# RetNet attention and a maxout FFN in one kernel: another order of the operand sums, and fewer of them between two plain products

## The chip, the cores and the metric

The kernel runs on one core of a Trainium2 chip. The metric is the device time of one execution in microseconds (us); a kernel's time is the median of several runs. The core has a matrix engine (TensorE, PE in the profile; its weight loads are listed as PEld), a vector engine (VectorE, DVE), a scalar engine (ScalarE, ACT), a general engine (GpSimd, POOL) and a queue engine that starts most transfers (SyncE, SP). Each engine works through its own instructions in the order in which the program gives them; between engines, and within one where a value is passed on, they wait on semaphores.

## What is computed

Eight sequences of 576 positions with 8 heads of 64 go through a retention step (scores with a decay by distance, no softmax). Its result, 4608 rows of 512, goes through a feed-forward layer whose hidden value is the largest of three products.

```python
scores = scale * np.matmul(q, k.transpose(0, 1, 3, 2))
ret = scores * Dmat[None, :, :, :]             # Dmat = gamma ** (i - j) for j <= i, else 0
x = (ret @ v) as (B*S, H*D)                    # 4608 x 512
h = np.maximum(np.maximum(x @ w1, x @ w2), x @ w3)   # 4608 x 768
out = h @ w_out                                # 4608 x 512
```

The four weights come in as 64-bit floats and are turned into 32-bit ones on the chip.

## The kernel before

Rows are handled in 36 chunks of 128, and four chunks make a tile of 512 rows; there are nine tiles, t = 0 to 8. While the feed-forward layer of tile t is computed (`ffn(t)`, a generator), the attention of tile t + 1 is worked in between (`steps(t + 1)`, a list of twelve stations; after each the generator goes on to its next `yield`). The order of the instructions on each engine is thus written out by the program.

The hidden value has six blocks (`fb`, 128 columns each), in three pairs (`fp`).

- Tile 0 uses plain products: `up_plain` (L610) makes x times one weight for one block; the first of three is copied to h by ScalarE (L615), the others are joined by a maximum on VectorE (L614). The output is made by `downs_plain` (L597). The weights are converted along the way.
- Tiles 1 to 8 use a scheme with fewer products: for each block, the 24 products of half-size operands are replaced by 20 products of *sums* of operands (`PRODUCTS`, L65, matmuls at L587). They form five chains A to E that add up in five PSUM banks' tiles: A and B take turns in one pair of banks (`ps_x`), E, C and D in another pair (`ps_y`), so that C of a block takes the bank used two before it, and D the bank of E. ScalarE copies the running values out (L572), VectorE joins them (L567).
- In tile 1 the blocks run in the order 2, 3, 0, 1, 4, 5, and blocks 2 and 3 are still plain (`plain`): the sums of the weights aren't ready. Block 3's plain products use `ps_y`.

The sums of operands are written as lists. `X_SUMS` (13 sums of parts a11 to a24 of x, once for each tile from 1 on) and `W_SUMS` (19 sums of parts b11 to b43 of the weights, once for each pair fp, in place or into n1 to n8) are worked one by one by `combine` (L346), each one VectorE operation on 128x256 values. A third set, the sums of w_out (`sums_of_outs`, L378), has three times two VectorE operations (L386, L387) and two POOL operations (L390, L391).

Two queues hold work that is given out bit by bit: `chores` (the sums of weights and of w_out) and `urgent` (what `soon` puts there from tile 1 on: masks of scores, sums of x, transposes, loads; and the sums of hidden values). `chore(n)` takes the next n entries, urgent ones first. `weight_sums(fp)` puts the 19 sums of a pair and one marker into `chores`; tile 1 begins with pairs 0 and 2 there, and pair 1 follows when blocks 2 and 3 are made. In the plain blocks of tile 1, `ffn` gives out a fixed number of chores after each of the three plain products:

```python
for step, cost in enumerate(steps_of_one):
    if fb in plain:
        chore(8)
```

`up_plain_all` has the maximum of a product right behind the product and ahead of these chores. In tile 0, after the down products of blocks 3, 4 and 5, `chore(2)` gives out the sums of w_out; a `yield` after blocks 1 and 3 lets the attention's stations in. The last of these holds the step that makes x of tile 1 (`values`, xT, L184), followed by the 13 sums of x.

Of the kernel before, what the change touches and what calls it, by code (L numbers as in the profile page):

```python
# [53 lines left out]
FILL = 224  # L54
PARTS = 20

X_SUMS = """s19 = a12 + a14, s15 = s19 - a22, s3 = a22 - a12, s10 = s3 - a13, s13 = a12 + a13, s20 = s10 + a23,
            s14 = a24 - s15, s11 = s20 + a24, s11 = a21 - s11, s7 = s11 - s13, s6 = s19 + s7,
            s16 = a11 - s11, s16 = s16 - a14"""
W_SUMS = """b33 = b13 + b33, n1 = b13 + b43, n2 = n1 - b41, n3 = b11 - n2, n4 = b33 - b32, b43 = b43 + n4,  # L60
            b23 = b43 - b23, b43 = b41 - b43, n5 = b22 + b23, b41 = b41 - n5, b21 = b21 - b41,
            b23 = b32 + b23, b22 = b22 - b21, b32 = b22 - b32, n6 = b31 + n2, n7 = b42 + n4,
            b42 = b42 - n5, b31 = b31 + b32, n8 = b12 - n4"""

PRODUCTS = """E a11 b12, E a14 b42, B s15 n5, A a22 b21, C s3 b23, B s19 b41, A s10 b32, C a13 b31, B s6 n2, A s13 b22,  # L65
              C a11 b11, B s14 n1, A s11 n4, D s7 b43, B a23 n6, A s20 b33, D s16 b13, B a21 n3, A a21 n8, A a24 n7"""
# [6 lines left out]
         "A7": [("A1", ("A1", "B6"), ALU.add), ("A1", ("A1", "A5"), ALU.max), ("hi", ("A1", "A7"), ALU.max)]}  # L73
X_SUMS, W_SUMS = ([x.split() for x in text.split(",")] for text in (X_SUMS, W_SUMS))
PRODUCTS = [x.split() for x in PRODUCTS.split(",")]
# [4 lines left out]
def kernel(  # L80
# [93 lines left out]
    def chore(n=1):  # L174
        for _ in range(n):
            if urgent or chores:
                (urgent or chores).popleft()()  # L177

    def soon(step):

        if spread:
            urgent.append(step)
        else:
            step()  # L184
# [34 lines left out]
    def transposes(g):  # L219
        both = qks[g] = {}  # L220
        if g >= BY_PE:
            for n in ("k", "q"):
                t = both[n] = att.tile([P, NP, C], FP32, tag=n + "T", name=n + "T", bufs=2 if n == "k" else 3)
                soon(partial(nc.vector.transpose, t[:].rearrange("a p c -> a (p c)"),
                             raws.pop(("kx" if n == "k" else n, g))[:].rearrange("a p b i -> a (p b i)")))
            return
        for n, src in (("k", raws["k", g]), ("q", raws.pop(("q", g)))):
            pool, tag = (ps_r, "r") if g >= CPT else (ps_x, "x")
            pt = pool.tile([P, NP, C], FP32, tag=tag, name=n + "t")
            for p in range(NP):  # L230
                nc.tensor.transpose(pt[:, p, :], pair(src, p), ident[:C, :C])
            t = both[n] = att.tile([P, NP, C], FP32, tag=n + "T", name=n + "T", bufs=2 if n == "k" else 3)
            nc.scalar.copy(t[:], pt[:])
# [88 lines left out]
    def output(chunks, o, t, i):  # L322
# [9 lines left out]
        if i == CPT - 1 and t > 0:  # L332
# [4 lines left out]
            def step(n, dst, _, a, sign, b):  # L337
                combine(*(xS[t][x] for x in (dst, a, b)), sign)
                if dst not in (later[0] for later in X_SUMS[n + 1:]):
                    made[t].add(dst)  # L340

            for n, line in enumerate(X_SUMS):
                soon(partial(step, n, *line))

    def combine(dst, a, b, sign):
        nc.vector.tensor_tensor(dst, a, b, op=ALU.add if sign == "+" else ALU.subtract)  # L346
# [191 lines left out]
    def weight_sums(fp):  # L538

        def step(dst, a, sign, b):  # L540
            combine(*(factor(n, slice(2 * fp, 2 * fp + 2)) for n in (dst, a, b)), sign)

        for dst, _, a, sign, b in W_SUMS:
            chores.append(partial(step, dst, a, sign, b))
        chores.append(partial(summed_fp.add, fp))

    def late_room():
        pool = late["pool"]
        late["W"] = [pool.tile([P, NF, P], FP32, name=f"n{n}") for n in range(1, 9)]
        late["X"] = {n: pool.tile([P, NH], FP32, name=n)[:] for n in sorted({x[0] for x in X_SUMS})}  # L550

    converting = convert_all()

    def convert(n):
        for _ in range(n):
            next(converting, None)
# [35 lines left out]
    def downs_plain(t, h):  # L592

        ps = [(ps_x, ps_y)[m % 2].tile([P, DM], FP32, tag="xy"[m % 2], name="down") for m in range(NT // P)]
        for fb in range(NF):
            for m, b in enumerate(ps):
                nc.tensor.matmul(b[:], lhsT=h[:, fb, m * P:(m + 1) * P], rhs=w_sb["out", fb],  # L597
                                 start=(fb == 0), stop=(fb == NF - 1))
                if fb == NF - 1:
                    osb = opool.tile([P, DM], FP32, tag="osb", name="osb")  # L600
                    nc.scalar.copy(osb[:], b[:])
                    nc.sync.dma_start(out[t * NT + m * P:t * NT + (m + 1) * P, :], osb[:])
            yield

    def up_plain(t, h, fb, i):
        ps = (ps_x, ps_y)[fb % 2].tile([P, NT], FP32, tag="xy"[fb % 2], name="up")
        first_of_all = t == 0 and (fb, i) == (0, 0)
        for cols in (slice(0, NT - C), slice(NT - C, NT)) if first_of_all else (slice(0, NT),):
            for dc in range(NDC):
                nc.tensor.matmul(ps[:, cols], lhsT=w_sb[i, fb][:, dc * P:(dc + 1) * P], rhs=xT[t][:, dc, cols],  # L610
                                 start=dc == 0 and cols.start == 0, stop=dc == NDC - 1,
                                 skip_group_check=first_of_all)
        if i > 0:
            return lambda: nc.vector.tensor_tensor(h[:, fb, :], h[:, fb, :], ps[:], op=ALU.max)  # L614
        return lambda: nc.scalar.copy(h[:, fb, :], ps[:])  # L615

    def ffn(t):

        h = hpool.tile([P, NF, NT], FP32, tag="h", name="h")
        if t == 0:  # L620
            for fp, i in units:
                for fb in (2 * fp, 2 * fp + 1):
                    maximum = up_plain(t, h, fb, i)
                    if CPT not in qks:
                        maximum()
                        transposes(CPT)
                        convert(4)
                        continue
                    convert(4)
                    maximum()  # L630
                yield
            convert(6)
            for fb, _ in enumerate(downs_plain(t, h)):
                convert(4 if fb < 2 else 4 * len(pieces))
                if fb == 2:
                    while_converting.close()
                    late["pool"] = ctx.enter_context(tc.tile_pool(name="late", bufs=1))
                    late_room()
                    sums_of_outs()
                elif fb > 2:  # L640
                    chore(2)
                if fb in (1, 3):
                    yield
            yield
            return
        if t == 1:
            spread.append(True)
            weight_sums(0)
            weight_sums(2)
        plain = (2, 3) if t == 1 else ()  # L650
        order = (2, 3, 0, 1, 4, 5) if t == 1 else (0, 1, 4, 5, 2, 3)
        total = sum(24 if fb in plain else len(PRODUCTS) for fb in order)
        count = parts = 0
        for n, fb in enumerate(order):
            if fb not in plain:
                while fb // 2 not in summed_fp:
                    chore()
            steps_of_one = up_plain_all(t, h, fb) if fb in plain else up(t, h, fb)
            for step, cost in enumerate(steps_of_one):
                if fb in plain:  # L660
                    chore(8)
                elif step % 2 or step % 5 == 4:
                    chore(len(urgent) > 0)
                elif step % 4 == 2 and chores:
                    chores.popleft()()
                count += cost or 1
                if count * (NF // 2 * 3) >= (parts + 1) * total:
                    parts += 1
                    yield
            if n % 2:  # L670
                sums_of_hidden(h, fb // 2)
                if fb in plain:
                    weight_sums(fb // 2)
        chore(len(urgent))
        for n, _ in enumerate(downs(t, h)):
            chore(4)
            if n in (1, 3):
                yield
        yield

    def up_plain_all(t, h, fb):
        for i in range(3):
            up_plain(t, h, fb, i)()
            yield 8
# [85 lines left out]
    for t in range(N // NT):  # L770
        work = ffn(t)
        for todo in steps(t + 1):
            for step in todo:
                step()
            next(work, None)
# [51 lines left out]
```

## Time and profile before

| | |
|---|---|
| median of 7 runs | 777.7 us (777.42 to 778.01) |
| the profiled execution | 777.75 us, span 776.0 us |
| granted TensorE clock | 0.999 |
| TensorE matmuls | 767.3 us busy, 5032 instructions |
| VectorE | 568.2 us busy, 1249 instructions |
| ScalarE | 325.9 us busy, 811 instructions |
| GpSimd | 102.0 us busy, 124 instructions |
| tile 0 | to about 123.4 us of the span |
| plain blocks of tile 1 | 123.4 to 146.2 us |

The span runs from the first to the last instruction of the program. Lines of the profile name a kernel line (L346), an engine, an operation, and the tiles that are written and read. In a list by time the first number is the start in us, the second the length; "x2" joins instructions that follow each other, and brackets give the idle time just before and what ended it. In a list of waits the numbers are the total in us, the times and the longest. Lines on one source line list the count and the shortest, median and longest duration in ns. Starts on VectorE can overlap the end of the instruction before by some 0.08 us, so the distance from start to start is what an instruction costs there.

### The profile page before, as it was taken

To read this page: it belongs to the slowest core of one execution; us is meant where nothing else is said; L and a number is where in the kernel's file an instruction comes from. 1 tells how busy PE (TensorE), PEld (TensorE's weight loads), DVE (VectorE), ACT (ScalarE), POOL (GpSimd) and SP (SyncE) were. 2 spreads that over 40 slices of the span, in tenths; PEclk is the share of its full clock that TensorE was granted. 3 is DMA by queue.
4 is the path that set the end of the run, shared out by engine and by line. 5 is a ranking of instruction groups with operands and counts; after the bars stand their busy time and mean duration, and the time that the engine had idled before them with its cause. 6 is when DMAs were issued, how large, how long until landed. Compare 5 with 4: busy or idle time off the path is not lost.

```text
span 776.0 us, 14508 instructions
## 1 busy us (share of the span) xinstructions
PE 767.3 (99%) x5032; PEld 626.3 (81%) x5032; DVE 568.2 (73%) x1249; ACT 325.9 (42%) x811; POOL 102.0 (13%) x124
## 2 busy tenths in 40 slices
PE   8999999999999999999999999999999999999998
PEld 7545454688888888888888888888888888888887
DVE  3998979889677857785769657875778567855672
ACT  3665631154154514452345234532544054524651
POOL 2210112111102201111111111110111001200000
PEclk9999999999999999999999999999999999999999
DMA  9995543333233332343223333333333324001001
GB/s 221 238 233 129 158 112 102 58 58 59 85 57 58 58 75 54 60 82 65 61 54 59 58 96 59 56 60 95 58 56 58 77 50 77 6 15 41 2 1 54
DMA packets 237082, 59.33 MB, mean 76 GB/s; under 512 B 217936, under 2 KB 235728, under 8 KB 237008
## 3 DMA queue, kind: packets, MB, share of 16 engines
q1 hardware_dynamic: 236432, 58.07, 34.7%
q8 instruction: 39, 0.64, 0.4%
q10 hardware_dynamic: 576, 0.33, 0.1%
q14 instruction: 35, 0.29, 0.1%
HBM read 48.89 MB, written 9.44 MB: 75 GB/s over the span
## 4 chain that ended last, share of the span: by engine, by line
PE 93%; DVE 4%; DMA 2%; SPq 1%; issue 0%; ACT 0%; DVEq 0%; ACTq 0%
PE a L587 18%; PE b L587 15%; PE dx L427 11%; PE up L610 8%; PE c L587 8%; PE dz L427 5%; PE d L587 5%; PE e L587 5%; PE s L242 4%; PE o L298 4%; PE dy L427 3%; PE down L597 2%; PE o L311 2%; PE kv L262 2%; DVE w L346 1%; DMA qraw<-in_q_dram 1%
## 5 line engine op out<-in xcount | busy, mean ns | idle before, releaser
L567 DVE TENSOR_TENSOR part<-part 128x256 f32<-128x256 f32 x460 | 207.8, 460 | 80.2 <-ACT part L572 72.5
L572 ACT COPY part<-a 128x256 f32<-128x256 f32 x276 | 102.7, 372 | 85.0 <-PE a L587 73.1
L572 ACT COPY part<-b 128x256 f32<-128x256 f32 x230 | 85.6, 372 | 125.5 <-PE b L587 113.7
L610 PE MATMUL up<-xT,w 128*128 128x512 f32 (+2 forms) x200 | 84.7, 578 | 0.7 <-DVE w L516 0.7
L213 POOL TENSOR_TENSOR vd<-vraw,gk 128x512 f32<-128x512 f32 x36 | 40.8, 1132 | 325.6 <-DMA vraw<-in_v_dram 155.4
L587 PE MATMUL a<-s,w 128*128 128x256 f32 x276 | 82.3, 380 | 0.0
L587 PE MATMUL b<-s,n 128*128 128x256 f32 x276 | 82.1, 379 | 0.0
L610 PEld LDWEIGHTS up<-xT,w 128*128 128x128 f32 x200 | 36.8, 190 | 42.8 <-issue 38.7
L587 PEld LDWEIGHTS b<-s,n 128*128 128x128 f32 x276 | 52.4, 190 | 7.1
L587 PEld LDWEIGHTS a<-s,w 128*128 128x128 f32 x276 | 52.3, 190 | 7.3 <-issue 0.2
L587 PE MATMUL c<-xT,w 128*128 128x256 f32 x184 | 56.0, 386 | 0.0
L587 PE MATMUL b<-xT,n 128*128 128x256 f32 x184 | 55.4, 382 | 0.0
L587 PE MATMUL d<-s,w 128*128 128x256 f32 x184 | 55.2, 382 | 0.0
L587 PE MATMUL e<-xT,w 128*128 128x256 f32 x184 | 47.2, 379 | 0.0
L587 PE MATMUL a<-xT,n 128*128 128x256 f32 x184 | 47.2, 379 | 0.0
L567 DVE TENSOR_TENSOR h<-part 128x256 f32<-128x256 f32 x92 | 42.2, 458 | 6.6
L427 PE MATMUL dx<-To,H 128*128 128x256 f32 (+1 forms) x204 | 44.9, 370 | 0.0
L434 ACT COPY part<-dx 128x256 f32<-128x256 f32 (+1 forms) x34 | 10.5, 363 | 80.1 <-PE dx L427 77.9
L177 DVE TENSOR_TENSOR xT<-o,gq 128x512 f32<-128x512 f32 x28 | 18.1, 686 | 33.4 <-PE o L311 33.4
L427 PEld LDWEIGHTS dx<-To,H 128*128 128x128 f32 x204 | 36.6, 190 | 5.5 <-issue 1.0
L271 POOL TENSOR_TENSOR state<-state,gs 128x256 f32<-128x256 f32 x24 | 18.4, 765 | 170.3 <-DVE state L270 170.3
L242 PEld LDWEIGHTS s<-qT,kT 64*128 64x128 f32 x576 | 33.8, 188 | 7.9 <-PE b L587 4.0
(104 smaller groups left out, 1301.9 us busy)
## 6 DMA issues: line engine op xcount, KB each, us to landing
bits<-in_moe_w_dram SPq DMA_DIRECT2D x36, 256.0 KB, 5.1
out_dram<-osb SPq DMA_DIRECT2D x35, 256.0 KB, 2.1
kraw<-in_k_dram SPq DMA_DIRECT2D x32, 256.0 KB, 2.9
vraw<-in_v_dram SPq DMA_DIRECT2D x32, 256.0 KB, 3.4
qraw<-in_q_dram SPq DMA_DIRECT2D x464, 16.0 KB, 1.8
kxraw<-in_k_dram SPq DMA_DIRECT2D x464, 16.0 KB, 1.8
bits<-in_moe_w_out_dram SPq DMA_DIRECT2D x6, 512.0 KB, 4.2
qraw<-in_q_dram SPq DMA_DIRECT2D x6, 256.0 KB, 4.7
```

What stands on the lines that cost most here:

```text
L177: (urgent or chores).popleft()()
L213: nc.gpsimd.tensor_tensor(t[:], raws.pop(("v", g))[:], gk[:].unsqueeze(2).to_broadcast([C, H, D]), op=ALU.mult)
L242: nc.tensor.matmul(s[j][:, p, :], lhsT=kT[r, p, :], rhs=qT[r, p, :], start=True, stop=True)
L262: nc.tensor.matmul(kvs[g][half(h % 2), h // 2, :], lhsT=kr[r:, h, :], rhs=vds[g][r:, h, :], start=True, stop=True)
L271: nc.gpsimd.tensor_tensor(t[:], t[:], gs[:], op=ALU.mult)
L298: nc.tensor.matmul(o[n % 2][half(c), m, n // 2, :], lhsT=vds[g][:, h, :], rhs=sts[g][:, h % 2, h // 2, :], start=m == 0 and n < 2, stop=be ...
L311: nc.tensor.matmul(o[n % 2][half(c), m, n // 2, :old], lhsT=states[g][r, h // 2, :], rhs=qks[g]["q"][r, h // 2, :old], start=False, stop=True,
L427: nc.tensor.matmul(o, lhsT=hS[n](fp)[:, m * P:(m + 1) * P], rhs=late["T"][n][:, fp, cols], start=first and fp == 0 and (m == 0 or last and ...
L567: nc.vector.tensor_tensor(out, a, b, op=op)
L572: nc.scalar.copy(t[:], ps[step[0]][:])
L587: nc.tensor.matmul(ps[chain][:], lhsT=factor(w, fb), rhs=xS[t][x], start=n == 1, stop=ends, skip_group_check=True)
L610: nc.tensor.matmul(ps[:, cols], lhsT=w_sb[i, fb][:, dc * P:(dc + 1) * P], rhs=xT[t][:, dc, cols], start=dc == 0 and cols.start == 0, stop= ...
```

## The change

The entries of both lists are put in another order; the same 13 and 19 sums are made. In tile 0 the six entries of the sums of w_out are given out as 4, 0 and 2 after blocks 3, 4 and 5, where it was 2, 2 and 2. In tile 1, after the second plain product of block 3 (the last plain product but one), 4 chores are given out in place of 8.

```diff
-X_SUMS = """s19 = a12 + a14, s15 = s19 - a22, s3 = a22 - a12, s10 = s3 - a13, s13 = a12 + a13, s20 = s10 + a23,
-            s14 = a24 - s15, s11 = s20 + a24, s11 = a21 - s11, s7 = s11 - s13, s6 = s19 + s7,
-            s16 = a11 - s11, s16 = s16 - a14"""
-W_SUMS = """b33 = b13 + b33, n1 = b13 + b43, n2 = n1 - b41, n3 = b11 - n2, n4 = b33 - b32, b43 = b43 + n4,
-            b23 = b43 - b23, b43 = b41 - b43, n5 = b22 + b23, b41 = b41 - n5, b21 = b21 - b41,
-            b23 = b32 + b23, b22 = b22 - b21, b32 = b22 - b32, n6 = b31 + n2, n7 = b42 + n4,
-            b42 = b42 - n5, b31 = b31 + b32, n8 = b12 - n4"""
+
+X_SUMS = """s19 = a12 + a14, s3 = a22 - a12, s15 = s19 - a22, s10 = s3 - a13, s13 = a12 + a13, s20 = s10 + a23,
+            s14 = a24 - s15, s11 = s20 + a24, s11 = a21 - s11, s7 = s11 - s13, s16 = a11 - s11, s6 = s19 + s7,
+            s16 = s16 - a14"""
+W_SUMS = """b33 = b13 + b33, n1 = b13 + b43, n4 = b33 - b32, n2 = n1 - b41, b43 = b43 + n4, n3 = b11 - n2,
+            b23 = b43 - b23, n7 = b42 + n4, n5 = b22 + b23, b43 = b41 - b43, b41 = b41 - n5, b23 = b32 + b23,
+            b21 = b21 - b41, b42 = b42 - n5, b22 = b22 - b21, n6 = b31 + n2, b32 = b22 - b32, n8 = b12 - n4,
+            b31 = b31 + b32"""
...
                     late_room()
                     sums_of_outs()
                 elif fb > 2:
-                    chore(2)
+                    chore({3: 4, 4: 0, 5: 2}[fb])
                 if fb in (1, 3):
                     yield
...
             for step, cost in enumerate(steps_of_one):
                 if fb in plain:
-                    chore(8)
+                    chore(4 if (fb, step) == (plain[-1], 1) else 8)
                 elif step % 2 or step % 5 == 4:
                     chore(len(urgent) > 0)
```

## The prediction

> **What bounds the kernel now.** I read first the busy times of the page, then TensorE's waits.
>
> ```profile
> span 776.0 us, 14508 instructions
> PE 767.3 (99%) x5032; PEld 626.3 (81%) x5032; DVE 568.2 (73%) x1249; ACT 325.9 (42%) x811; POOL 102.0 (13%) x124
> ```
>
> TensorE (PE) is busy for 767.3 of 776.0 us. A VectorE (DVE) saving is worth only what it takes off a TensorE wait, so the list of these waits (total, times, longest) says what can be won at all:
>
> ```profile
> PE c L587 <- DVE h L614: 1.6, 1, 1.6
> PE warm L147 <- POOL ident masks.py:199: 1.4, 1, 1.4
> PE o L298 <- POOL vd L213: 1.1, 1, 1.1
> PE up L610 <- DVE w L516: 0.7, 1, 0.7
> ```
>
> Only the first has to do with the change; the others lie ahead of 116 us, where no sum of w or x has run yet. It is the first product of chain C of tile 1 waiting for the last maximum (L614) of the plain products: C takes the bank that this maximum reads. TensorE there (start, length):
>
> ```profile
> 147.46 0.59 PE L587 MATMUL a<-xT,w 128*128 128x256 f32 x2
> 149.62 0.70 PE L587 MATMUL c<-s,w 128*128 128x256 f32 x2 [1.56 <-DVE h L614]
> 150.15 0.59 PE L587 MATMUL b<-s,w 128*128 128x256 f32 x2
> ```
>
> From a to the next b are 2.69 us. The same three products of the next block start at 161.54 (a) and 162.41 (b): 0.87 us. So the stall costs **1.82 us**: the 1.56 of the wait, the overlap that is lost and 0.1 for the first pass after it.
>
> Why was the maximum late? VectorE and GpSimd (POOL) in time order:
>
> ```profile
> 144.17 1.28 DVE L177 TENSOR_TENSOR st<-s,causal 128x512 f32<-128x512 f32 x2
> 145.37 0.42 DVE L346 TENSOR_TENSOR w<-w,w 128x256 f32<-128x256 f32 x1
> 145.82 0.43 DVE L346 TENSOR_TENSOR w<-w 128x256 f32<-128x256 f32 x1
> 146.16 1.60 DVE L346 TENSOR_TENSOR n<-w,n 128x256 f32<-128x256 f32 x2
> 147.80 0.83 DVE L346 TENSOR_TENSOR w<-w,n 128x256 f32<-128x256 f32 x1
> 148.55 0.41 DVE L346 TENSOR_TENSOR w<-w,w 128x256 f32<-128x256 f32 x1
> 148.89 0.67 DVE L614 TENSOR_TENSOR h<-h,up 128x512 f32<-128x512 f32 x1
> ```
>
> ```profile
> 146.36 1.12 POOL L213 TENSOR_TENSOR vd<-vraw,gk 128x512 f32<-128x512 f32 x1 [16.96 <-DMA vraw<-in_v_dram]
> 147.45 0.90 POOL L404 TENSOR_TENSOR H<-h 128x256 f32<-128x256 f32 x1
> ```
>
> VectorE runs without a gap from 116.51 to 149.6 and is behind. The eight chores put after the last plain product but one are two masks (st) and six sums; the maximum stands behind them, and two of the six are stretched, to 1.27 (the second n) and 0.83 us, beside POOL's two operations.
>
> **When the maximum must begin.** C's weight load came 0.05 us after the maximum's end (149.56, 149.61). Without a wait it would start 0.43 after that of a, at 147.24 + 0.43 = 147.67. So the maximum, 0.67 long, must begin by 146.95: 1.94 us earlier. It cannot begin before its product is there. The plain product begun at 123.38 was copied (L615) at 127.01, 3.63 later; the last one's first pass is at about 142.73 (16 passes from 139.19 to 146.16), so it is ready at 146.36. That leaves 0.6 us of room.
>
> **The change part by part.**
>
> *The cut from 8 to 4 chores.* The two masks and two sums stay ahead of the maximum, four sums go behind it. Their time is 146.16 to 148.89: 2.73 us. The maximum could then begin at 146.16 by VectorE's queue, so its product sets it: 146.36, end 147.03, C's load not held at 147.67. This part alone takes the whole stall away. What is moved comes after: five sums instead of one stand between the maximum and what follows (H, then the join of E, L567). At 0.34 to 1.27 us each these are 1.7 to 6.4 us; I take 2.7 + 0.3, the rows' own sum, so the join of E ends near 150.8 at most. Who waits for it is chain D, which takes E's bank: its first product is at 157.23 now, 155.41 when 1.82 earlier. 4.6 us of cover; 1.3 at the upper end. No other engine waits on the five: their weights belong to blocks 4 and 5, which come behind blocks 0 and 1.
>
> *The order of the sums.* A sum that takes its neighbour's result costs more, start to start:
>
> ```profile
> 117.72 0.41 DVE L346 TENSOR_TENSOR s<-xT 128x256 f32<-128x256 f32 x1
> 118.17 0.43 DVE L346 TENSOR_TENSOR s<-s,xT 128x256 f32<-128x256 f32 x1
> 118.51 0.42 DVE L346 TENSOR_TENSOR s<-xT 128x256 f32<-128x256 f32 x1
> ```
>
> 0.45 us into the dependent one (s15 after s19), 0.34 into the free one: 0.11 for each such pair. Overwriting what the neighbour reads costs the same (b43 = b41 - b43 behind b23: 131.43 to 131.89). Results two back cost nothing (134.09 and the next, b22, both free of it). By the lists, X_SUMS goes from 6 such pairs to 2 (s11 and s7 remain), 0.44 us in tile 1; W_SUMS from 8 to 1 (b41 overwrites what b43 = b41 - b43 reads), 0.77 us a round, and one round and 14 sums of a second, holding all 8, lie ahead of the maximum: 1.5. Together some 2.0 us of VectorE, between 0 (should the pipeline empty either way) and 2.0. None of it is on the path once the cut has been made: the product sets the maximum. In the later tiles TensorE waits for no sum: those of the second tile end at 210.14 and are used from 211.52 on, and s15 and s6, the two that move back by a place, are done at 199.8 and 209.4 now; a place is 0.34.
>
> The Trainium skill's page "VectorE: DVE Perf Modes" (section "The DRAIN you can't avoid") speaks against this part: it says that the pipe empties after each operation whether or not a semaphore stands between, and that the semaphore costs nothing. By it the order saves 0 us of VectorE, and the time comes from the cut alone; the 0.45 against 0.34 here disagree.
>
> *The sums of w_out at t = 0 (2, 2, 2 becomes 4, 0, 2).* The second pair moves ahead of the values step: two VectorE operations (0.42 each, or 0.95 and 0.83 beside POOL) go from 124.37 into VectorE's 4.5 us idle ahead of xT at 116.51, from 112.0 to 113.8 at the latest. Two POOL operations (0.90, 0.91) go ahead of the state step into POOL's 10.04 us idle before 123.31. The one that overwrites part of w_out follows block 2's down products, some 3 us earlier. No DMA is moved, no load is passed. This clears 0.76 us from VectorE's full stretch, and up to 1.0 more where the third pair was stretched (125.13 to 126.87 for two). If that cover were gone, xT would be late by at most what is over 2.7 us: nothing. Taken at zero, being ahead of the same maximum.
>
> **The sum.** The profiled execution took 777.75 us (span 776.0 and 1.7 around it), 0.05 over the median of 777.7. 777.75 - 1.82 = 775.93, from the median 775.9. All later work of TensorE moves up with it. What is tied to other times has room: vd of 146.36 ends at 147.48 and is read by kv, 153.77 now and 151.95 then; kT and qT end at 160.7, scores begin at 180.40.
>
> **The rivals.**
>
> *Part of the stall stays.* If POOL's vd, beginning at 146.36 as the maximum would, held it to 147.48, it would end at 148.15 and C's load come at 148.20: 0.53 late and 0.1 for the first pass, a gain of 1.2, 776.5. For it: sums reading two SBUF tiles stretch to 1.27. Against: the maximum reads PSUM, and operations with such an operand do not stretch. All joins of e (shortest, median, longest in ns), then one join of c beside a vd in time order:
>
> ```profile
> L567 DVE TENSOR_TENSOR part<-e,part x46: 383/418/425, 150.2 to 749.1; 128x256 f32<-128x256 f32 x46
> ```
>
> ```profile
> 514.03 1.04 POOL L213 TENSOR_TENSOR vd<-vraw,gk 128x512 f32<-128x512 f32 x1 [9.46 <-PE a L587]
> 514.11 0.42 DVE L567 TENSOR_TENSOR part<-c,part 128x256 f32<-128x256 f32 x1
> ```
>
> 46 joins of e have a longest of 425 ns, and one of c kept 0.42 inside a vd. Chance 0.12.
>
> *The wait comes back later.* TensorE, 1.82 us ahead, meets a load or a vd at a fixed time: 777.7. Against it stand the 4.5 us and more above, and no TensorE wait after 150 us in the list. Chance 0.08.
>
> *Slower: the moved sums hold D.* Place: D's first product behind E's join. The join follows five sums, H (0.34) and itself (0.41). It decides once D comes after 155.41, that is once a sum takes over (155.41 - 0.75 - 147.03) / 5 = 1.5 us; slower than before by 0.2% needs D at 158.8, 2.2 us a sum. At 2.4 us, D is at 159.8, 4.4 late: 775.9 + 4.4 = 780.3. No sum in the trace is above 1.27. Chance 0.05.
>
> *The change doesn't do what it says:* the order saves nothing. The time stays 775.9, as the cut alone is enough.
>
> **How the numbers follow.** The whole stall gone: 0.75, its own range 775.5 to 776.2 (runs of one kernel spread by 0.3 either way). About 0.2%, 1.56 us, is what a measurement of this kernel can tell from no change, so faster means below 776.1; 0.04 of the 0.75 falls short of that. Faster 0.71, same 0.04 + 0.12 + 0.08 = 0.24, slower 0.05. The range from 775.4 to 776.8 holds the first case and most of the partial one.
>
> **What would show it.** Right: the wait of c for h is gone, the maximum begins near 146.4, a to b there takes 0.87, dependent pairs of sums are few and VectorE idles ahead of the last two maxima. Wrong: a wait of C or D for VectorE of over 0.3 us, a maximum longer than 0.7, or a new TensorE wait after 150 us.

## The result, and the profile after

The changed kernel takes 775.74 us (median of 16 runs), the kernel before 777.76 us over its runs beside it. The ratio is 0.9973, with a 95% interval of 0.9966 to 0.9979. The forecast was 775.9. The ratio is worked out from all runs of both kernels, so it need not be the quotient of the two medians; by it the gain is 1.6 to 2.6 us.

The page and TensorE's list of waits (total, times, longest) of the kernel after; its line numbers are one higher than before:

```profile
span 774.4 us, 14511 instructions
PE 766.6 (99%) x5032; PEld 626.1 (81%) x5032; DVE 564.7 (73%) x1249; ACT 325.8 (42%) x811; POOL 101.7 (13%) x124
```

```profile
PE qt L232 <- DMA qraw<-in_q_dram: 1.7, 2, 1.4
PE up L611 <- DVE w L517: 1.6, 1, 1.6
PE warm L148 <- POOL ident masks.py:199: 1.4, 1, 1.4
```

The wait of c for h is gone; what is left lies in tile 0. These waits add up to 4.7 us, where those of tile 0 in the profile before add up to 4.2, and tile 1 starts 0.20 us later (its first plain product at 123.58, before at 123.38). The span is 1.6 us shorter all the same. TensorE at the place of the old stall, in order of time:

```profile
147.66 0.59 PE L588 MATMUL a<-xT,w 128*128 128x256 f32 x2
148.09 0.59 PE L588 MATMUL c<-s,w 128*128 128x256 f32 x2
148.53 0.59 PE L588 MATMUL b<-s,w 128*128 128x256 f32 x2
```

From a to the next b are 0.87 us, as in the blocks behind; it was 2.69. Below, "the gap" is this distance less 0.87: 1.82 before, 0 after. VectorE and GpSimd around it:

```profile
143.20 0.69 DVE L615 TENSOR_TENSOR h<-h,up 128x512 f32<-128x512 f32 x1 [2.03 <-PE up L611]
143.81 1.28 DVE L178 TENSOR_TENSOR st<-s,causal 128x512 f32<-128x512 f32 x2
145.01 0.41 DVE L347 TENSOR_TENSOR w<-w 128x256 f32<-128x256 f32 x1
145.34 0.42 DVE L347 TENSOR_TENSOR w<-w,n 128x256 f32<-128x256 f32 x1
146.57 0.69 DVE L615 TENSOR_TENSOR h<-h,up 128x512 f32<-128x512 f32 x1 [0.81 <-PE up L611]
147.17 0.96 DVE L347 TENSOR_TENSOR w<-w,w 128x256 f32<-128x256 f32 x1
148.05 0.95 DVE L347 TENSOR_TENSOR n<-w,n 128x256 f32<-128x256 f32 x1
```

```profile
146.81 1.04 POOL L214 TENSOR_TENSOR vd<-vraw,gk 128x512 f32<-128x512 f32 x1 [19.42 <-DMA vraw<-in_v_dram]
147.81 0.91 POOL L405 TENSOR_TENSOR H<-h 128x256 f32<-128x256 f32 x1
```

VectorE now idles 2.03 and 0.81 us ahead of the last two maxima, until their products are there. The last maximum keeps its 0.69 us although vd begins inside it; the two sums behind it, which read two SBUF tiles, are the ones that vd and H stretch.

### The profile page after: what moved, and what is told of

Its sections match the earlier page's. It is cut to its first block, busy times and chain, and to the rows that moved or that the text cites. A ratio compares the mean times of both kernels' runs of the same rounds, so it can differ in the third digit from the quotient of the medians.

```text
span 774.4 us, 14511 instructions
## 1 busy us (share of the span) xinstructions
PE 766.6 (99%) x5032; PEld 626.1 (81%) x5032; DVE 564.7 (73%) x1249; ACT 325.8 (42%) x811; POOL 101.7 (13%) x124
## 4 chain that ended last, share of the span: by engine, by line
PE 98%; DVE 1%; DMA 1%; issue 0%; ACT 0%; POOL 0%; POOLq 0%; DVEq 0%
PE a L588 18%; PE b L588 16%; PE dx L428 11%; PE up L611 11%; PE c L588 8%; PE dz L428 5%; PE d L588 5%; PE e L588 5%; PE s L243 5%; PE o L299 4%; PE down L598 3%; PE dy L428 3%; PE kv L263 2%; PE o L312 2%; DMA qraw<-in_q_dram 1%; PE qt L232 0%
```

## The experiments

E is the first product behind the plain ones (a multiplication of chain E). "vd against E" is when vd starts, from E's start, in the profiled execution; the gap is of the same execution. The ratio to the kernel before is with its interval.

| kernel | vd against E, us | gap, us | median, us | ratio |
|---|---|---|---|---|
| before (first profile) | +0.20 | 1.82 | 777.76 | |
| before_again | +0.77 | 1.98 | 778.4 (one run) | |
| the change | +0.44 | 0 | 775.74 | 0.9973 (0.9966 to 0.9979) |
| cut_only | +0.03 | 0 | 775.8 | 0.9977 (0.9968 to 0.9986) |
| cut_half | -0.26 | 1.16 | 776.33 | 0.9981 (0.9972 to 0.9990) |
| order_only | +0.69 | 0 | 775.87 | 0.9982 (0.9973 to 0.9992) |
| wout_only | +0.61 | 0 | 776.78 | 0.9990 (0.9979 to 1.0001) |
| before_vd_late | +3.70 | 0.58 | 776.31 | 0.9977 (0.9966 to 0.9989) |
| order_vd_early | -3.29 | 0 | 775.78 | 0.9961 (0.9947 to 0.9974) |
| after_vd_early | -3.04 | 0 | 775.45 | 0.9961 (0.9947 to 0.9974) |
| order_vd_mid | -1.75 | 0.81 | 777.34 | 0.9992 (0.9983 to 1.0001) |
| all_but_cut_vd_mid | -1.53 | 1.01 | 776.99 | 0.9988 (0.9979 to 0.9997) |
| after_vd_mid | -2.02 | 0 | 776.1 | 0.9981 (0.9972 to 0.9989) |
| extra20 | | (at d) | 779.65 | 1.0016 (1.0005 to 1.0026) |

The kernel before was run again beside each group: its median was 777.76 beside the change, 777.83 beside the four that follow it in the table from cut_only on, 778.34 beside those with vd late or early and extra20, and 777.98 beside those with "mid" and before_again. So medians of different groups should not be compared to a few tenths; the ratios can be.

The gap is that of one execution, and single runs of one kernel spread by a us and more. The gap shows what happened in that execution, the median and the ratio what it is worth over many; where the two disagree, it is said below.

### Each part alone

**The cut alone** (against the kernel before):

```diff
-                    chore(8)
+                    chore(4 if (fb, step) == (plain[-1], 1) else 8)
```

> The kernel before with the cut alone: 4 chores in place of 8 behind the second plain product of block 3; both lists of sums and the sums of w_out as they were. My theory (what is queued ahead of the last maximum decides, and the cut alone takes 2.73 us off it where 1.94 are needed): TensorE's wait of c for h is gone, the last maximum begins when its product is there, about 0.2 us after the first product of E begins; 1.8 us less than before, 775.9. Rival (the order of the sums brings the time): 777.7, as before.

```profile
146.45 0.69 DVE L614 TENSOR_TENSOR h<-h,up 128x512 f32<-128x512 f32 x1
147.05 1.42 DVE L346 TENSOR_TENSOR n<-w,n 128x256 f32<-128x256 f32 x2
146.28 1.04 POOL L213 TENSOR_TENSOR vd<-vraw,gk 128x512 f32<-128x512 f32 x1 [16.80 <-DMA vraw<-in_v_dram]
```

775.8, no wait of c for h. The maximum begins at 146.45 with E at 146.25, so 0.20 behind E, as worked out, and keeps its 0.69 us although vd began 0.17 ahead of it. The sums are in their old order, and the two n still take 1.42 us together (1.60 before); they simply stand behind the maximum. The rival falls: the order isn't needed.

**Half the cut:**

```diff
-                    chore(8)
+                    chore(6 if (fb, step) == (plain[-1], 1) else 8)
```

> The kernel before with 6 chores in place of 8 behind the second plain product of block 3, so that only the last two sums of the eight chores go behind the last maximum. By the rows of before the maximum would begin at 147.80 in place of 148.89, 0.85 us later than C can bear: a wait of c for h of some 0.6 us stays, the gain is 0.9 us, 776.8. Rival (all or nothing: what is stretched beside GpSimd's vd is what made the maximum late, and it stays ahead): no gain, 777.7. Rival (any cut is enough): 775.9.

```profile
148.64 0.70 PE L587 MATMUL c<-s,w 128*128 128x256 f32 x2 [0.90 <-DVE h L614]
```

A wait of 0.90 and a gap of 1.16, so 0.66 of the 1.82 won in the profiled execution, where 0.9 was expected: vd came sooner against E than in the first profile, and the two n sums took 2.13 us together (1.60 before). The median (776.33) gives more, 1.5, with runs from 775.2 to 777.6; why, one profile doesn't show. In that profile neither all-or-nothing nor "any cut is enough" fits.

**The orders alone** (both lists as in the change, the rest as before):

> The kernel before with the new order of both lists of sums alone; 8 chores and the sums of w_out as they were. It saves some 2.0 us of VectorE ahead of the last maximum. My theory: TensorE sets the maximum before the last (at about 143.0, it was 143.58), so of what is saved ahead of that only 0.6 us comes through, and behind it only one pair's 0.11; the six sums still meet GpSimd's vd at 146.36. A wait of c for h of 0.3 to 0.6 us stays, gain 1.0 to 1.3, 776.4 to 776.7. Rival (all that VectorE saves comes through): 2.0 saved against 1.94 needed, wait gone, 775.9. Rival (the rule that each operation waits for the pipe to empty in any case): no saving, 777.7, and the starts of neighbouring sums 0.45 apart in both orders.

```profile
142.74 0.69 DVE L614 TENSOR_TENSOR h<-h,up 128x512 f32<-128x512 f32 x1 [1.44 <-PE up L610]
146.55 0.68 DVE L614 TENSOR_TENSOR h<-h,up 128x512 f32<-128x512 f32 x1
146.59 1.04 POOL L213 TENSOR_TENSOR vd<-vraw,gk 128x512 f32<-128x512 f32 x1 [17.94 <-DMA vraw<-in_v_dram]
```

775.87, no wait: a miss of my expectation. Half of the reasoning held: TensorE set the maximum before the last, VectorE idled 1.44 us there, and that saving was lost. What didn't hold is that a sum would meet vd. The six sums ran from 144.54 on with no stretch, and vd began at 146.59, 0.05 before the last of them ended. The profiled execution (775.51) is the second fastest of the 11, which reach to 778.45; what happened in the slow ones was not seen.

**The sums of w_out as 4, 0, 2 alone:**

```diff
-                    chore(2)
+                    chore({3: 4, 4: 0, 5: 2}[fb])
```

> The kernel before with the sums of w_out given out as 4, 0, 2 alone; orders and 8 chores as they were. VectorE is some 1.7 us ahead at the start of tile 1. My theory: TensorE sets the maximum before the last, so 0.6 us of it comes through to the six sums, and one of these meets GpSimd's vd all the same: gain 0.5, 777.2, a wait of c for h of about 1.0 to 1.3. Rival (all comes through): wait of 0.2, 776.0. Rival (worth nothing): 777.7.

```profile
146.59 0.42 DVE L346 TENSOR_TENSOR w<-w,w 128x256 f32<-128x256 f32 x1
146.64 1.27 POOL L213 TENSOR_TENSOR vd<-vraw,gk 128x512 f32<-128x512 f32 x1 [19.09 <-DMA vraw<-in_v_dram]
```

The median is 776.78, between my 777.2 and the rival's 776.0, and the interval reaches 1.0. The profiled execution (775.66, the second fastest of the 11) has no wait of c. Here vd did meet the sixth sum, but 0.05 us after that sum had begun: the sum kept its 0.42, and vd took 1.27 in place of 1.04. So the gap of 0 is not what the median stands for. A new question: do the orders or the sums of w_out remove the stall, or only when GpSimd's vd happens to come late?

### Moving vd

vd waits for a transfer (vraw of chunk 10) in SyncE's queue; where that load stands among the chunk's 32 small q and k loads sets vd's time without changing any other engine's list. For chunk 10, written shorter than in the kernels, with only the lines around v:

```diff
 # before_vd_late: v behind the first eight loads of chunk 11
+    load_blocks(11, 0); load_rows(10, "v"); load_blocks(11, 1, 2, 3); load_rows(11, "k", "v")
 # ..._vd_early: v ahead of the last four k loads (not shown); ..._vd_mid: ahead of the last two
+    load_blocks(10, 3, names=("kx",), parts=(0, 1)); load_rows(10, "v")
+    load_blocks(10, 3, names=("kx",), parts=(2, 3)); load_rows(10, "k")
```

**The kernel before, vd late:**

> The kernel before, with one transfer moved: the values v of chunk 10, on which GpSimd's vd near 146.4 us waits, are loaded behind the first block's eight q and k transfers of chunk 11 in place of ahead of them, 3.8 us later on SyncE's queue, so that vd comes near 150 us, behind the last maximum. Nothing of the change is in it. Theory (what makes the maximum as late as it is in the kernel before is to a good part that vd and then H stretch the sums ahead of it): none of the six sums ahead of the last maximum is stretched, it begins about 1.3 us sooner against E's first product, a wait of c for h of some 0.4 to 0.7 us stays, gain 1.0, 776.7. Rival (the stretch does not matter): 777.7 with the same wait of 1.6.

```profile
148.73 0.70 PE L606 MATMUL c<-s,w 128*128 128x256 f32 x2 [0.33 <-DVE h L633]
150.21 1.04 POOL L232 TENSOR_TENSOR vd<-vraw,gk 128x512 f32<-128x512 f32 x1 [20.45 <-DMA vraw<-in_v_dram]
```

With nothing of the change in it, the gap falls from 1.82 to 0.58 and the time to 776.31. None of the six sums is stretched now. So, from one profile to the other, 1.24 us of the stall were sums held by vd and H, and the rest was that there were too many of them. By the ratio the gain is 1.8 us, more than the gap shows and than the 1.0 expected; the difference is not explained.

**The orders alone, vd early:**

> The kernel with the new orders of the sums alone (8 chores, 2, 2, 2), and the values v of chunk 10 loaded ahead of the last four k transfers of that chunk, 2.4 us sooner, so that GpSimd's vd and H come near 144 to 146 us, beside the six sums ahead of the last maximum. Theory (that the orders alone took the wait away in the profiled execution hung on vd coming just behind the sixth sum): two or three of the six sums are stretched again, the last maximum begins 1.0 to 1.5 us later than with the orders alone, a wait of c for h of 0.5 to 1.0 is back, 776.6. Rival (the orders alone are enough whatever GpSimd does): 775.8 and no wait.

The load came sooner than I had worked out (vd at 143.00, 3.29 ahead of E, where 144 to 146 was wanted), and vd and H fell beside the maximum and the masks, which read PSUM. Nothing was stretched, no wait, 775.78. It missed its aim, and shows the harmless case.

**The whole change, vd early:**

> The whole change, with the same early load of the values v of chunk 10. Theory (the cut gives room: only two sums are left for vd and H to stretch): the two sums take up to 1.5 us more, and VectorE idled 0.8 us ahead of this maximum, so it begins at most some 0.5 us later; no wait of c for h above 0.2, 775.8, as the change itself. Rival (the change hangs on vd's time as much as the orders alone): 776.6.

The same: vd at 142.57, no wait, 775.45. Here too vd and H fell beside the maximum and the masks, so the two sums that are left were not put to the test. With only six runs and an interval that overlaps, it is not shown to beat the change itself.

**The orders alone, vd at the sums:**

> The new orders of the sums alone, with the values v of chunk 10 loaded ahead of the last two k transfers of that chunk, about 1.5 us sooner than in the kernel before, so that GpSimd's vd comes near 144.8 us, at the first of the six sums ahead of the last maximum (2.4 us sooner it had fallen beside the maximum and the masks, which read PSUM and did not stretch). Theory (the orders alone leave no room, and do without the wait only when vd misses the six sums): two of the six sums are stretched by 0.4 to 0.85 us each, the last maximum begins 1.2 us later against E's first product than with the orders alone, a wait of c for h of 0.5 to 1.0, 776.8. Rival (orders alone are enough whatever GpSimd does): no wait, 775.8.

```profile
145.67 0.94 DVE L363 TENSOR_TENSOR w<-w 128x256 f32<-128x256 f32 x1
146.53 0.94 DVE L363 TENSOR_TENSOR w<-w,n 128x256 f32<-128x256 f32 x1
149.46 0.70 PE L604 MATMUL c<-s,w 128*128 128x256 f32 x2 [0.55 <-DVE h L631]
```

vd begins 1.75 ahead of E, two sums take 0.94 each, and c waits again: a gap of 0.81, median 777.34, an interval that reaches 1.0. The orders alone were enough only as long as vd held none of the sums.

**The change without its cut, vd at the sums:**

> The whole change without the cut (8 chores again; new orders; sums of w_out as 4, 0, 2), with the same load of v of chunk 10. Theory (what VectorE saves ahead of the last maximum but one is lost there, since TensorE sets that one): as with the orders alone under the same load, a wait of c for h of 0.5 to 1.0, 776.8; the last maximum but one begins after VectorE idled about 2 us. Rival (the saved time adds up): no wait, 775.8.

```profile
144.40 0.69 DVE L632 TENSOR_TENSOR h<-h,up 128x512 f32<-128x512 f32 x1 [2.04 <-PE up L628]
150.21 0.70 PE L605 MATMUL c<-s,w 128*128 128x256 f32 x2 [0.75 <-DVE h L632]
```

VectorE idles 2.04 us ahead of the maximum before the last: adding the earlier sums of w_out only lengthens this idle time. The gap is 1.01, the median 776.99, against the rival that savings add up.

**The whole change, vd at the sums:**

> The whole change with the same load of v of chunk 10, vd near 144.8 us. Theory (the cut leaves two sums there and 0.8 us of idle time): both may be stretched, the last maximum begins at most 0.7 us later against E, where 0.6 is the room: wait of c for h 0 to 0.2, 775.8. Rival (hangs on vd as the orders alone do): 776.8.

```profile
145.74 0.66 DVE L364 TENSOR_TENSOR w<-w 128x256 f32<-128x256 f32 x1
146.33 0.94 DVE L364 TENSOR_TENSOR w<-w,n 128x256 f32<-128x256 f32 x1
147.30 0.69 DVE L632 TENSOR_TENSOR h<-h,up 128x512 f32<-128x512 f32 x1
```

Both sums that are left are stretched, and the maximum still begins 0.20 behind E (147.10), when its product is there. No wait; 776.1. The second sum ended 0.03 us ahead of the maximum, so VectorE's idle time was used up; what is left is the 0.59 us by which C can bear a later maximum. Of the three kernels with this load only the one with the cut has no gap, though the intervals of their ratios overlap. A vd some 0.6 us later would be worse: by an estimate from these rows (vd just ahead of the first sum, 1.4 ahead of E, then H, and a sum that ends 0.28 after H) the maximum would begin some 0.7 behind E, still inside the 0.79 that C can bear. That place was not run.

**The kernel before, once more:**

> The kernel before once more, for a second profile: how far does vd's start move against E's first product from one execution to the next, and with it the wait of c for h? Theory: vd's start lies 0.2 us behind E's in the first profile and within 0.7 either way here; the wait is 0.6 to 1.8 and the time moves with it. Rival (the wait is 1.6 in every execution).

```profile
147.51 1.29 DVE L346 TENSOR_TENSOR w<-w,n 128x256 f32<-128x256 f32 x1
148.72 0.94 DVE L346 TENSOR_TENSOR w<-w,w 128x256 f32<-128x256 f32 x1
150.32 0.70 PE L587 MATMUL c<-s,w 128*128 128x256 f32 x2 [1.72 <-DVE h L614]
```

vd came 0.77 behind E, not 0.20, and stretched the fifth and sixth sum in place of the fourth and fifth; the wait was 1.72. Over all profiles with the load in its old place vd moves from -0.26 to +0.77. In the kernel before, the six sums begin between 0.8 us ahead of E and over 2 us behind it, so vd met some of them in both profiles.

### The price of work behind the last maximum

```diff
+                    if (fb, step) == (plain[-1], 2):
+                        spare = [ppool.tile([P, NH], FP32, tag="part", name="part") for _ in range(2)]
+                        for r in range(20):
+                            nc.vector.tensor_tensor(spare[r % 2][:], xS[t]["a11"], xS[t]["a12"], op=ALU.add)
```

> The whole change with 20 more VectorE sums of two parts of x into two spare tiles right behind the five sums that follow the last maximum; nothing uses their values. It tests the price and the cover of work moved behind that maximum. Theory (chain D's first product waits for the join of E, with 4.7 us of cover): at 0.34 us each the 20 take 6.7 us, the join of E ends near 157.4, D's weight load comes 2.0 us late, a wait of d for the join (part, L568) of about 2 us, 775.7 + 2.1 = 777.8. Rival (TensorE waits for something sooner, such as the masks or the copies): more than 4 us, 780. Rival (the work is hidden in full, as VectorE idles later): 775.8.

```profile
159.34 0.70 PE L588 MATMUL d<-s,w 128*128 128x256 f32 x2 [1.68 <-DVE part L568]
169.95 0.70 PE L588 MATMUL d<-s,w 128*128 128x256 f32 x2 [1.71 <-DVE part L568]
```

779.65, 3.9 us over the change's median, or 3.3 when each is set against the kernel before beside it (1.0016 and 0.9973). The place is the expected one, chain D behind E's join, and the first delay too: 157.07 (a) to 159.34 is 2.27 in place of 0.43, 1.84 and 0.1 for the first pass. What I left out is a second wait of the same size in the next block (1.71): VectorE had not caught up by then; its list shows no idle time from 149.07 to 171 us. Behind both waits the work is 3.9 us later against E than in the change (the next block's E 24.81 behind E, there 20.89). The profiled execution is the slowest of its kernel, 781.81; of its 5.7 us over the profiled change, 1.9 lie ahead of tile 1 (its first plain product is at 125.48, in the change at 123.58).

## Why the prediction was right

- **The price of the stall.** 1.82 from a to b, not the 1.56 of the wait line: the gap is 0 after, and chain D's first product moved from 157.23 to 155.60, 1.63 sooner with a tile 1 that began 0.20 later, so 1.83. The medians fell by 2.0. That the forecast of 1.8 came so close has some luck in it: it took the stall of one profile, and the second profile of the same kernel has 1.98.
- **When the maximum can begin.** Worked out as 146.36 with E at 146.16. It is 146.57 with E at 146.37, the same 0.20 behind.
- **The cut alone is enough.** Shown by cut_only. That the last maximum is not held by vd is shown by its 0.69 there, with vd begun 0.17 ahead of it. The rival that part of the stall stays had that as its mechanism.
- **The five sums behind.** Taken as 3.0 us with E's join ending near 150.8; they took 147.17 to 149.93, 2.76, and the join ended at 150.67. Chain D did not wait. The slower rival's place was right, but it sized a late D too low: a VectorE that is 2 us late there costs 3.9, not 2.
- **The order.** 13 sums of x take 117.92 to 122.53, 4.61, where they took 117.72 to 122.82, 5.10: 0.49 saved, 0.44 worked out. The starts of sums (the third and fourth, then two of which the second depends on the first):

```profile
118.59 0.75 DVE L347 TENSOR_TENSOR s<-s,xT 128x256 f32<-128x256 f32 x2
120.27 0.42 DVE L347 TENSOR_TENSOR s<-s,xT 128x256 f32<-128x256 f32 x1
120.72 0.42 DVE L347 TENSOR_TENSOR s<-xT,s 128x256 f32<-128x256 f32 x1
```

  s15 and s10, free of each other, are 0.33 apart by the joined 0.75; the second sum into s11 (a21 - s11) comes 0.45 behind the first, on which it depends. For the weights, the first 12 sums of the second round took 4.89 before (137.49 to 142.38) and take 4.16 now (135.73 to 139.89). W_SUMS has a ninth pair that the prediction left out (b42 overwrites what n7 reads, 0.46 in the run with vd late); it stands behind the 14 sums counted there.

  The Trainium skill's page "VectorE: DVE Perf Modes" (section "The DRAIN you can't avoid") measured eight copies that took the same time with and without a semaphore between them. For these sums what the neighbour reads does matter, 0.45 against 0.33, so what the prediction took from the page, 0 us saved, does not hold here; whether the 0.11 is a semaphore or the emptying of the pipe, the runs don't tell. The same section also says that a next operation that isn't held (made to wait until those before it have finished) starts earlier, which the prediction left out; the sums free of each other, which start 0.08 us before their neighbour ends, agree with it.
- **The sums of w_out.** The second pair ran from 112.13 to 113.94 in the idle time, and kT of the next chunk begins at 124.88 in place of 126.87: 2.0 sooner, 2.2 against the tile's start, as 0.49, 0.76 and the 1.0 that was named as an upper end.
- **What was too simple.** I set the orders and the sums of w_out at zero beside the cut, and that was so. But for each alone I counted on vd at 146.36; with the load untouched it moved by a microsecond against E, and both parts alone did without the wait in their profiled executions. The prediction did not hang on it: the maximum was not stretched, and the sums that vd could hold stood behind it.

## What to carry to other kernels

Here the stall of the busy engine was decided by what another engine had queued ahead of one instruction, back to the last point where the busy engine itself set the pace; time saved before that point turned into idle time there. Moving work behind the instruction gained at least as much as making it cheaper, and of the variants tried it alone held when GpSimd's operation fell on the queued work. Before moving it, look for the next one that waits, and count its cover and whether the queue catches up before the one after.

## What the runs showed of the hardware

- GpSimd's vd and H stretched VectorE sums of two SBUF tiles from 0.42 to between 0.66 and 1.29 us, and never the maxima or masks, which read PSUM (0.68 to 0.69 beside vd).
- A sum held by vd or H ended 0.28 us after it, whatever its start: in the profile after, vd ends at 147.85 and the sum at 148.13, H at 148.72 and the next sum at 149.00; in the second profile of the kernel before, 148.52 and 148.80, 149.38 and 149.66. So a held sum's length follows from the end of GpSimd's operation.
- Which of the two began first decided who was longer. A sum that was running when vd began kept its 0.42, and vd took 1.27 (the sums of w_out alone) or 1.25 (half the cut) in place of 1.04.
- The start of an operation that waits for a transfer moved by 1.0 us against TensorE's work between profiles of kernels with the same loads, and by 0.57 between two profiles of one kernel. That such a shift decides the stall is shown where the load was moved; that it does so between runs of one kernel was not seen.
